# Routing attention and a hard-swish FFN on one core: band steps, the last pair's slots, two loads and an output queue rearranged

## The chip, the core and the metric

One core of a Trainium2 chip runs the kernel. TensorE (PE) multiplies matrices and writes to PSUM, VectorE (DVE), ScalarE (ACT) and GpSimd (POOL) work on tiles, SyncE (SP) issues DMAs; ACT and POOL issue some as well. Each engine takes its instructions in the order in which the program lists them, and waits where one needs what another engine or a DMA has not yet delivered. The metric is the device time of one execution in microseconds (us), as a median of several runs.

## The reference

```python
batch, n_heads, seq, head_dim, n_clusters = 4, 8, 768, 64, 16
q_assign = argmax(einsum('bhsd,hcd->bhsc', q_n, c_n), axis=-1)     # nearest centroid of each query
k_assign = argmax(einsum('bhsd,hcd->bhsc', k_n, c_n), axis=-1)     # and of each key
mask = q_assign[..., :, None] == k_assign[..., None, :]
scores = where(mask, q @ k.T / sqrt(64), -1e9)
attn = softmax(scores) @ v                                          # (4, 8, 768, 64)
x = attn.transpose(0, 2, 1, 3).reshape(3072, 512)
h = x @ w_in                                                        # (3072, 2048)
out = (h * clip(h + 3, 0, 6) / 6) @ w_out                           # (3072, 512)
```

A query attends to the keys of its own cluster only; then a feed-forward network runs over all 3072 tokens. All is float32.

## The kernel before

The 32 heads are worked on as 16 pairs (two heads of 64 dimensions fill 128 partitions). Four pairs make a batch of the attention's output, and a batch of the FFN can start when its four pairs are done.

**First part, the main loop.** Pairs 0 to 6 are computed in full width: a loop over steps `n` (two at a time, 12 to a pair) issues scores (L423, PE), exponentials (L446, ACT), sums over the keys (L454 and L457, POOL) and the product with v (L467, PE). In the same loop the FFN's weights are loaded as raw 512 KB pieces on SP's queue (`load_weights`, L232) and decoded (`decoding_steps`, L245 to L276, on ACT and DVE); each piece's `split` asks for the piece two further on. When batch 0's four pairs are done, their key sums are inverted and the first FFN block is loaded: `load_sums` appends `invert` and then `complete` to the list `later`, which is run once in each turn of the loop, and `complete` calls `load_block`, which issues the block's x (`xb`, L577) and its inverse sums (`rb`, L581) on SP. `divide` (L531, DVE) multiplies the two; the first `ph` matmuls (L656) need its result.

**Second part, the plan of items.** Pairs 7 (`FIRST`) to 15 go another way. Their tokens are ranked by cluster, the rows of q, k and v are scattered to DRAM in ranked order, and then only a band about the diagonal has to be computed. For each pair `steps_of` lists steps with an offset, and `late_plan` puts each step at item `i = 38 + 29 * (pair - 8) + offset`. The steps in question are

- ranking: `load_natural`, `turn_natural`, `cluster_scores`, `own_clusters`, `run_up`, `step_up` (L1071, DVE), `order` (L1106, L1119, PE), `positions`, and `scatter` (L1155, indirect DMAs that POOL issues);
- band: `load_ranked`, `turn_ranked`, three `band_scores` (L1228, PE; exponentials at L1250 and L1264, ACT), two `band_values` (L1285, PE), `key_adds` (L1299, DVE), `band_sums` (`pd`, L1309, PE, copied to `dn` by ACT at L1314), `band_divide` (`pdt` at L1322 and `ps` at L1326 on PE, then DVE);
- back in natural order: `keep_ranked` (L1343, SP), `gather` (L1198, twelve indirect DMAs on POOL), and `turn_back`, which transposes the gathered rows (`turn_piece`, L1038, PE), copies them to `xt` (L1039, ACT) and stores them to DRAM (L1353, SP).

After the steps of item `i` the loop issues one half-item of the FFN from the list `fill`, but none where `(i - 38) % 29` is 6 or 9. `turn_back` of a batch's last pair adds that batch's FFN items to `fill`.

**The FFN.** Each of the 4 batches has 3 blocks of 256 tokens, each block 8 `up` items and 7 `down` items of two halves. In `up`, `uX` (first half) and `uY` (second half) are matmuls at L709, with precomputed sums of weights `tx` that ACT's queue loads (L595, 384 KB) two items ahead; ACT and DVE then make the gate (L538, L541, L699, L720, L727). In `down`, `X` and `Y` are matmuls at L748; DVE adds the parts (L755) and `keep` (L761) writes the output in pieces of 128 KB, on SP's queue unless it is told otherwise.

**Buffers that matter.** In the second part the PSUM pool `psum_s` has a single buffer, which `turn_back` (L1038), `band_scores` (L1228) and `band_divide` (L1326) share. The pool `rowp` (tiles `xn`, `bn`, `xr`, `xt`) has three buffers.

**The end.** After the last step of the plan, `turn_back(15)`, `st["last"]` is set, `whether_good` puts a chain of small checks on DVE, and the rest of `fill` runs: what is left of batch 2, then batch 3.

Of the kernel before, what the change touches and what calls it, by code (L numbers as in the profile page):

```python
# [16 lines left out]
B, H, S, D = 4, 8, 768, 64  # L17
# [7 lines left out]
NPAIR = NG // 2  # L25
# [21 lines left out]
FIRST = NPAIR // 2 - 1  # L47
# [78 lines left out]
def fast_path(ctx, tc, ok, q, k, v, centroids, moe_w_in, moe_w_out, out):  # L126
# [380 lines left out]
    def load_sums(b):  # L507
        size = 2 * NCH
        tok = plain[:, NKT * b * size : (NKT * b + unsorted(b)) * size]
        nc.sync.dma_start(tok, st["sums", b].rearrange("k t s -> (k t s)").rearrange("(p n) -> p n", p=P))  # L510

        def invert():
            nc.vector.reciprocal(out=tok, in_=tok)
            nc.sync.dma_start(st["rd", b].rearrange("k t s -> (k t s)").rearrange("(p n) -> p n", p=P), tok)
            return complete

        def complete():
            if unsorted(b) == NKT:
                waiting.extend((b, m) for m in range(NHC))
                load_block()  # L520

        if b == 0:
            later.append(lambda: later.append(lambda wait=invert(): later.append(wait)))
        else:
            st["invert"], st["complete"] = invert, complete

# [108 lines left out]
    def ffn_items(b):  # L635
# [121 lines left out]
        def down(m, part):  # L757
# [33 lines left out]
            def end():  # L791
                multiply(1)
                if part == 0:
                    finish()
                    st["gating"] = False
                if (b, m, part) == (B - 1, NHC - 1, 6):
                    st["good"] = nc.values_load(ok[0:1, 0:1], min_val=0, max_val=1)
                if part == 4:
                    token_sums(*divmod(b * NHC + m + 1, NHC))
                y0, y1 = st["y0"], st.get("y1")  # L800
                if part == 1:
                    nc.scalar.copy(out=y0[:, HC:], in_=st["X"][:, HC:])
                    add(y0[:, HC:], y0[:, HC:], st["X"][:, 0:HC])
                elif part == 3:
                    add(y1[:, 0:HC], y0[:, HC:], st["Y1"][:, HC:])
                    add(y1[:, HC:], y1[:, 0:HC], st["Y"][:, 0:HC])
                    keep(1, 1, y1[:, HC:])
                elif part == 4:
                    nc.scalar.copy(out=y0[:, 0:HC], in_=st["X"][:, 0:HC])
                    keep(0, 0, y0[:, 0:HC])  # L810
                elif part == 5 and closing:
                    z = sxp.tile([P, 4, P], F32, name="sx").rearrange("p k c -> p (k c)")[:, 0:HC]
                    add(z, y0[:, HC:], st["Y"][:, 0:HC])
                    keep(0, 1, z)
                elif part == 6:
                    add(y1[:, 0:HC], y0[:, HC:], st["Y1"][:, HC:])
                    keep(1, 0, y1[:, 0:HC])
                    if not closing:
                        add(y0[:, HC:], y0[:, HC:], st["Y"][:, 0:HC])
                        keep(0, 1, y0[:, HC:], nc.scalar if st["last"] else nc.sync)  # L820
                if (b, m) == (0, 0):
                    for i in ([HF - 1, HF - 2], [5], [4], [], [3, 2], [0], [1])[part]:
                        make_first_sums(i)
                    if part in (0, 1):
                        weight_sums(6 + part)
                    elif part in (2, 3):
                        weight_sums(2 + part)
# [114 lines left out]
    def open_late():  # L942
# [2 lines left out]
        late = ctx.enter_context(ExitStack())  # L945
        for name, bufs in (
            ("rankp", 1), ("piecep", 2), ("svp", 1), ("fromp", 1), ("sortp", 1), ("bandp", 2), ("edgep", 1),
            ("wholep", 1), ("rowp", 3), ("posp", 3),
        ):
            st[name] = right(late, name, bufs)  # L950
        for name, bufs in (("psum_y", 2), ("psum_s", 1)):
# [409 lines left out]
    def steps_of(g):  # L1361

        first, last = g == SECOND, g == NPAIR - 1
        if first:
            plan = [
                (-38, load_queries), (-38, load_keys, 0), (-38, load_keys, 1),
            ]
        elif g == FIRST:
            plan = [(-6, lambda g: st.pop("signed")())]
        else:  # L1370
            plan = [
                (-52, load_natural, 1), (-51, load_natural, 0), (-46, turn_natural, 1), (-45, turn_natural, 0),
                (-42, cluster_scores), (-40, own_clusters), (-39, load_queries), (-39, run_up), (-38, step_up),
                (-36, load_keys, 0), (-35, order), (-34, positions), (-33, load_keys, 1),
            ]
        s = -37 if first else -30
        if g == FIRST:
            plan += [
                (-5, load_ranked, 0), (-4, load_ranked, 1), (-3, load_ranked, 2), (-5, band_masks),
                (-1, turn_ranked, 0), (0, turn_ranked, 1),  # L1380
            ]
        else:
            plan += [
                (s, scatter, 0), (s, scatter, 1), (-12, band_masks), (-9, load_ranked, 0),
                (-7, load_ranked, 1), (-6, load_ranked, 2), (-4, turn_ranked, 0), (-3, turn_ranked, 1),
            ]
        if last:
            plan += [
                (1, band_scores, (0, 5), 1), (2, band_scores, (2,), 3), (3, band_scores, (4,)),
                (3, band_values, 0), (3, key_adds, 0, 1, 2), (4, key_adds, 0, 3), (5, band_values, 1),  # L1390
                (5, key_adds, 1, 1, 2), (6, key_adds, 1, 3), (8, band_sums), (9, band_divide), (10, keep_ranked),
                (11, gather), (24, turn_back),
            ]
        else:
            plan += [
                (2, band_scores, (0, 5), 1), (4, band_scores, (2,), 3), (6, band_scores, (4,)),
                (6, band_values, 0), (6, key_adds, 0, 1, 2), (7, key_adds, 0, 3), (9, band_values, 1),
                (9, key_adds, 1, 1, 2), (10, key_adds, 1, 3), (12, band_sums), (14, band_divide), (16, keep_ranked),
                (17 if g == FIRST else 23, gather), (37, turn_back),
            ]  # L1400
        return [(g, *step) for step in plan]

    def late_plan():

        at = {}
        for g in range(FIRST, NPAIR):
            for _, offset, op, *args in steps_of(g):
                i = (AHEAD + SLOT * (g - SECOND) - 2 * (g == NPAIR - 1) if g > FIRST else 6) + offset
                assert i >= 0, (g, offset)
                at.setdefault(i, []).append((op, g, *args))  # L1410
        return [at.get(i, []) for i in range(max(at) + 1)]
# [85 lines left out]
    with tc.manual_schedule():  # L1497
# [24 lines left out]
        for n in range(0, total + lag_d + 2, 2):  # L1522
# [19 lines left out]
                prep.pop(0)()  # L1542
            if r == 6:
                load(g + 2, "q", "k")
                load(g + 1, "v")
            if len(prep) > 1:
                prep.pop(0)()
# [410 lines left out]
```

## Time and profile before

| | us |
|---|---|
| median of 3 runs | 925.34 |
| lowest, highest | 924.95, 927.41 |
| the profiled execution | 924.17 |
| its span | 922.4 |
| PE busy in it | 895.6 |
| POOL, DVE, ACT busy in it | 600.1, 586.4, 305.0 |
| mean granted clock of PE | 0.996 |

The profile shows one execution. Its page gives for each engine the busy time and its share of the span. Further views list what each engine waited for and for how long; the instructions in order of time, with the idle time before each in brackets and whoever ended it; the clock granted to PE in any window; and the chain of work that ended last. A row such as `PE ps L1038` names the engine, the tile written and the line. PE weight loads (PEld) overlap the matmuls, and so do neighbouring matmuls a little.

### The profile page before, as it was taken

Reading aid. Unit: us, or ns where it says so; the run is one execution under the profiler, and the core shown is the slowest. Engines: PE = TensorE matmul, PEld = TensorE weight load, DVE = VectorE, ACT = ScalarE, POOL = GpSimd, SP = SyncE. Lnnn points to the kernel's source line nnn. Section 1 sums busy time; section 2 is a strip of 40 time slices with the busy share of each in tenths; the row PEclk is TensorE's granted clock in tenths of the full one; section 3 lists DMA queues with packets and bytes.
Section 4 is the critical chain, followed back from the end, with each engine's and each line's share of the span. In section 5 each row is a group of like instructions: output and inputs, shape, how many; then the busy total and the mean of one; then the engine's idle time right before and its main releaser. Section 6 shows DMA issues by size and latency. Waiting matters only on the chain.

```text
span 922.4 us, 17421 instructions
## 1 busy us (share of the span) xinstructions
PE 895.6 (97%) x6131; PEld 701.4 (76%) x6131; DVE 586.4 (64%) x1373; ACT 305.0 (33%) x627; POOL 600.1 (65%) x1438
## 2 busy tenths in 40 slices
PE   8999999999999999999999999999999988999997
PEld 5444444657798797887977978978888878999996
DVE  5874898799787394693774855856744716445361
ACT  6888786651220322212222230321412201112120
POOL 3878899996867858787888777787886051203030
PEclk9999999999999999999999999999999999999999
DMA  6656666536769577593792954937635413233220
GB/s 178 169 154 170 174 186 186 160 98 136 199 165 197 134 182 152 151 238 89 185 216 79 223 110 140 236 102 172 160 108 132 122 42 111 88 83 102 63 64 28
DMA packets 248377, 131.06 MB, mean 142 GB/s; under 512 B 206972, under 2 KB 225816, under 8 KB 248280
## 3 DMA queue, kind: packets, MB, share of 16 engines
q1 hardware_dynamic: 224168, 81.22, 36.9%
q10 hardware_dynamic: 13744, 34.44, 13.5%
q0 software_dynamic: 10368, 14.18, 5.1%
q8 instruction: 51, 0.84, 0.4%
q14 instruction: 46, 0.38, 0.1%
HBM read 99.82 MB, written 29.97 MB: 141 GB/s over the span
## 4 chain that ended last, share of the span: by engine, by line
PE 48%; DVE 9%; DMA 4%; POOL 2%; issue 1%; ACT 1%; ACTq 0%; SPq 0%; DVEq 0%; POOLq 0%
PE Y L748 14%; PE uY L709 9%; PE X L748 9%; PE uX L709 8%; PE pv L1285 3%; PE ps L1228 2%; DMA tx<-td 2%; DVE g_sb L720 1%; DVE sx L720 1%; DVE g_sb L699 1%; DVE g_sb L541 1%; POOL xn L1198 1%; PE pv L1228 1%; PE pd L1309 1%; PE ps L1038 1%
## 5 line engine op out<-in xcount | busy, mean ns | idle before, releaser
L1198 POOL DMA_INDIRECT xn<-xsd,pos x108 | 106.7, 988 | 58.9 <-DMA xsd<-xr 29.3
L538 ACT ACTIVATE sx<-g_sb,half_c 128x512 f32<-128x512 f32 x88 | 63.6, 722 | 198.5 <-DVE g_sb L720 198.3
L1147 POOL MEMSET unread<- 128x1 f32 x972 | 102.3, 105 | 37.6
L699 POOL TENSOR_TENSOR g_sb<-g_sb 128x256 f32<-128x256 f32 x52 | 39.6, 783 | 118.7 <-DVE g_sb L541 117.6
L457 POOL TENSOR_TENSOR acc<-acc,ex 128x768 f32<-128x768 f32 x56 | 104.5, 1867 | 16.7 <-ACT ex L446 14.1
L1155 POOL DMA_INDIRECT qd<-qn,pos x96 | 98.1, 1022 | 20.0 <-issue 14.4
L1155 POOL DMA_INDIRECT kvd<-kvn,pos x96 | 95.5, 995 | 21.8 <-issue 21.8
L748 PE MATMUL X<-w_out_sb,g_sb 128*128 128x256 f32 x384 | 93.3, 387 | 1.5 <-DVE g_sb L541 1.4
L709 PE MATMUL uX<-xb,w_in_sb 128*128 128x128 f32 x704 | 93.0, 275 | 0.0
L748 PE MATMUL Y<-T,g_sb 128*128 128x256 f32 x384 | 88.5, 381 | 0.0
L748 PE MATMUL Y<-w_out_sb,g_sb 128*128 128x256 f32 x384 | 88.5, 381 | 0.0
L709 PEld LDWEIGHTS uX<-xb,w_in_sb 128*128 128x128 f32 x704 | 85.7, 192 | 0.0
L748 PEld LDWEIGHTS X<-w_out_sb,g_sb 128*128 128x128 f32 x384 | 71.7, 193 | 16.3 <-DVE g_sb L541 3.9
L748 PEld LDWEIGHTS Y<-w_out_sb,g_sb 128*128 128x128 f32 x384 | 72.2, 190 | 12.6 <-issue 2.7
L748 PEld LDWEIGHTS Y<-T,g_sb 128*128 128x128 f32 x384 | 72.0, 190 | 12.5 <-issue 2.7
L755 DVE TENSOR_TENSOR y<-y,Y 128x256 f32<-128x256 f32 x47 | 19.7, 420 | 92.7 <-PE Y L748 91.9
L720 DVE TENSOR_TENSOR sx<-uX,sx 128x128 f32<-128x128 f32 x176 | 50.7, 288 | 38.3 <-ACT sx L727 34.1
L423 PE MATMUL ps<-xf 64*128 64x384 f32 x336 | 68.8, 487 | 0.6 <-ACT ex L446 0.6
L720 DVE TENSOR_TENSOR g_sb<-uY,sx 128x128 f32<-128x128 f32 (+1 forms) x176 | 65.5, 413 | 0.2 <-DVE sx L720 0.2
L446 ACT ACTIVATE ex<-ps 128x768 f32<-128x768 f32 x84 | 63.7, 803 | 3.1 <-PE ps L423 2.6
L541 DVE SCALAR_TENSOR_TENSOR g_sb<-sx,g_sb 128x512 f32<-128x512 f32 x88 | 63.3, 722 | 2.0 <-ACT sx L538 2.0
L467 PE MATMUL pv<-ex,vt 128*64 128x384 f32 x336 | 63.5, 499 | 0.0
(228 smaller groups left out, 1723.7 us busy)
## 6 DMA issues: line engine op xcount, KB each, us to landing
tx<-td ACTq DMA_DIRECT2D x86, 384.0 KB
raw<-in_moe_w_in_dram SPq DMA_DIRECT2D x16, 512.0 KB
raw<-in_moe_w_out_dram SPq DMA_DIRECT2D x16, 512.0 KB
xb<-xd SPq DMA_DIRECT2D x12, 512.0 KB
out_dram<-y SPq DMA_DIRECT2D x44, 128.0 KB
piece<-qd SPq DMA_DIRECT2D x36, 96.0 KB
piece<-kvd SPq DMA_DIRECT2D x36, 96.0 KB
vs<-kvd SPq DMA_DIRECT2D x18, 192.0 KB
```

The costliest lines, as they stand in the source:

```text
L423: nc.tensor.matmul(st["ps", n][:, t, 0:HALF], lhsT=x[r, NCH + j], rhs=x[r, hf * NHC : (hf + 1) * NHC], start=first, stop=last, skip_group_ ...
L446: nc.scalar.activation(out=ex, in_=sc, func=ACT.Exp, scale=SM_SCALE)
L457: nc.gpsimd.tensor_tensor(out=acc, in0=acc, in1=ex, op=ALU.add)
L467: nc.tensor.matmul(pv[t * D : (t + 1) * D], lhsT=vt[:, t, j], rhs=ex[:, t], start=(j == 0), stop=(j == NCH - 1),)
L538: nc.scalar.activation(out=r, in_=h, func=ACT.Relu, bias=half_c, scale=1.0 / 6.0)
L541: nc.vector.scalar_tensor_tensor(out=g, in0=r, scalar=1.0, in1=h, op0=ALU.min, op1=ALU.mult)
L709: nc.tensor.matmul(dst, lhsT=w[:, kt], rhs=x(kt), start=(kt == 0), stop=(kt == HK - 1))
L720: nc.vector.tensor_tensor(out=out_, in0=in0, in1=in1, op=ALU.add)
L748: nc.tensor.matmul(bank[:, half * HC : (half + 1) * HC], lhsT=g_sb[:, kind, i], rhs=w[:, i], start=(first and i == 0), stop=(last and i == ...
L1147: nc.gpsimd.memset(unread, 0.0)
L1155: i = nc.gpsimd.indirect_dma_start(out=rows[name, g, t], in_=src[:, j, t].rearrange("p a d -> p (a d)") if a else src[:, j, t], in_offset= ...
L1198: nc.gpsimd.indirect_dma_start(out=xn[:, j, t], out_offset=None, in_=rows["xsd", g, t], in_offset=bass.IndirectOffsetOnAxis(ap=pos[:, 0, j ...
```

## The change

- The first block's loads: `invert` and `complete` of batch 0 go one level deeper into `later`, so that `complete`, and with it the loads of `xb` and `rb`, runs one turn of the loop later.
- `load(g + 1, "v")` runs at `r == 8` of a pair instead of `r == 6`.
- The output half (0, 1) of a block's last part goes to ACT's queue if its batch is the last, and not whenever the plan has ended.
- `rowp` has four buffers.
- Pair 8's base is 35 instead of 38, with offsets changed so that its loads and scatter stay where they were; its other steps come three items sooner.
- Pairs 9 to 15: the ranking up to `step_up` comes one item sooner; `load_queries`, `load_keys`, `order`, `positions` and `scatter` stay.
- All pairs but the last: `band_sums` at 11 (was 12), `band_divide` at 13 (was 14), `keep_ranked` at 14 (was 16), pair 7's `gather` at 15 (was 17), `turn_back` at 35 (was 37).
- The last pair: its steps with an offset above -20 are shifted by -4, where all its steps were shifted by -2; those before lose that shift. `turn_back(15)` gets offset 26 instead of 24 and stays at the same item.

```diff
         if b == 0:
-            later.append(lambda: later.append(lambda wait=invert(): later.append(wait)))
+            later.append(lambda: later.append(lambda wait=invert(): later.append(lambda: later.append(wait))))
...
-                        keep(0, 1, y0[:, HC:], nc.scalar if st["last"] else nc.sync)
+                        keep(0, 1, y0[:, HC:], nc.scalar if b == B - 1 else nc.sync)
...
-            ("wholep", 1), ("rowp", 3), ("posp", 3),
+            ("wholep", 1), ("rowp", 4), ("posp", 3),
...
         if first:
             plan = [
-                (-38, load_queries), (-38, load_keys, 0), (-38, load_keys, 1),
+                (-35, load_queries), (-35, load_keys, 0), (-35, load_keys, 1),
             ]
...
-                (-52, load_natural, 1), (-51, load_natural, 0), (-46, turn_natural, 1), (-45, turn_natural, 0),
-                (-42, cluster_scores), (-40, own_clusters), (-39, load_queries), (-39, run_up), (-38, step_up),
+                (-53, load_natural, 1), (-52, load_natural, 0), (-47, turn_natural, 1), (-46, turn_natural, 0),
+                (-43, cluster_scores), (-41, own_clusters), (-40, run_up), (-39, load_queries), (-39, step_up),
                 (-36, load_keys, 0), (-35, order), (-34, positions), (-33, load_keys, 1),
             ]
-        s = -37 if first else -30
+        s = -34 if first else -30
...
         if last:
...
-                (11, gather), (24, turn_back),
+                (11, gather), (26, turn_back),
             ]
         else:
             plan += [
                 (2, band_scores, (0, 5), 1), (4, band_scores, (2,), 3), (6, band_scores, (4,)),
                 (6, band_values, 0), (6, key_adds, 0, 1, 2), (7, key_adds, 0, 3), (9, band_values, 1),
-                (9, key_adds, 1, 1, 2), (10, key_adds, 1, 3), (12, band_sums), (14, band_divide), (16, keep_ranked),
-                (17 if g == FIRST else 23, gather), (37, turn_back),
+                (9, key_adds, 1, 1, 2), (10, key_adds, 1, 3), (11, band_sums), (13, band_divide), (14, keep_ranked),
+                (15 if g == FIRST else 23, gather), (35, turn_back),
             ]
...
-                i = (AHEAD + SLOT * (g - SECOND) - 2 * (g == NPAIR - 1) if g > FIRST else 6) + offset
+                i = offset + {FIRST: 6, SECOND: 35}.get(g, AHEAD + SLOT * (g - SECOND))
+                if g == NPAIR - 1 and offset > -20:
+                    i -= 4
...
             if r == 6:
                 load(g + 2, "q", "k")
+            if r == 8:
                 load(g + 1, "v")
```

## The prediction

> **What bounds the kernel now.** I read the page's first part, then the list of waits for TensorE (PE), then the timeline around each long wait, then clock and busy time by windows.
>
> ```profile
> span 922.4 us, 17421 instructions
> PE 895.6 (97%) x6131; PEld 701.4 (76%) x6131; DVE 586.4 (64%) x1373; ACT 305.0 (33%) x627; POOL 600.1 (65%) x1438
> ...
> PE ps L1038 <- DMA xn<-xsd,pos: 3.4, 3, 1.2
> ...
> PE ps L423 <- ACT ex L446: 2.9, 4, 2.1
> PE rk L1106 <- DVE upto L1071: 2.5, 3, 1.4
> ...
> PE ps L1228 <- ACT be L1250: 0.3, 1, 0.3
> ```
>
> The last four rows are: engine and line, what it waited for, us in total, times, longest. PE is busy for 895.6 of 922.4 us, so 26.8 us idle are all that a reordering can win, and PE's instructions stay the same 6131. A wait taken from PE shortens the run by its length, a new one lengthens it; what DVE (VectorE), ACT (ScalarE), POOL (GpSimd) and the DMAs do counts only where PE waits for it. The sum goes against this profiled execution, 924.17 us (its span and 1.77 us around it). The median of the runs, 925.34, is 1.17 above it; I add the difference that I find to the median.
>
> **The change part by part.** One ended wait is worth a little more than the row says: two neighbouring PE pieces overlap (the row 728.13 0.82 below ends at 728.95, the next starts at 728.79), so 0.16 us of overlap come back with it.
>
> *A, first block later.* The x and 1/sum loads of the first block (xb, rb) go behind two raw weight loads on SP's queue.
>
> ```profile
> 131.06 0.38 SPq L232 DMA_DIRECT2D raw<-in_moe_w_out_dram  x1
> 131.97 0.53 SPq L577 DMA_DIRECT2D xb<-xd  x1
> 134.82 3.97 SPq L232 DMA_DIRECT2D raw<-in_moe_w_out_dram  x2
> 144.08 0.67 ACT L245 ACTIVATE wsize<-raw 128x512 bf16<-128x512 f32 x1 [2.82 <-DMA raw<-in_moe_w_out_dram]
> 145.49 1.22 DVE L531 TENSOR_TENSOR xb<-xb,rb 128x1024 f32<-128x1024 f32 x1
> 145.59 0.34 PE L423 MATMUL ps<-xm 64*128 64x384 bf16 x2 [2.13 <-ACT ex L446]
> 149.54 1.78 PE L656 MATMUL ph<-xb,w_in_sb 128*128 128x256 f32 x7
> ...
> raw<-in_moe_w_out_dram SPq DMA_DIRECT2D x5, 512.0 KB
> xb<-xd SPq DMA_DIRECT2D x1, 512.0 KB
> rb<-rd SPq DMA_DIRECT2D x2, 256.0 KB
> ...
> xd<-num SPq DMA_DIRECT2D x2, 192.0 KB
> ```
>
> Times are us from the span's start; in brackets the idle time before and who ended it. The raw load issued at 134.82, behind xb and rb, reaches ACT only at 144.08; the exponentials queued behind it on ACT come late, and PE stands 2.13 us. With both raw loads first that ends: −2.3 with the overlap. What is late next is the first block. From 131.06 to 144.08 the queue brought raw, the 192 KB of xd, xb, rb and raw, 2240 KB in 13.0 us, or 3.0 us for 512 KB. The second raw load, issued by 138.79, is in at about 141.5, xb and rb 6.0 us later, at 147.5. The division (1.22 us) ends at 148.7, while the first `ph`, now at 149.54, would be due 2.3 earlier, at 147.25. So it waits 1.4: A = −0.9. Bounds: −2.3 if the loads are quicker, +2.1 if another 512 KB lie ahead of them. Queued behind the division on DVE is the decoding of weights, for which ACT and the next raw load wait; that is inside the upper bound.
>
> *B, ranking one item sooner.* `run_up` and `step_up` (DVE) go ahead of the half-item after which `order` (PE) stands.
>
> ```profile
> 286.69 0.25 PE L1106 MATMUL rk<-every,upto 128*128 128x1 bf16 x4 [1.37 <-DVE upto L1071]
> 402.42 0.25 PE L1106 MATMUL rk<-every,upto 128*128 128x1 bf16 x4 [0.45 <-DVE upto L1071]
> 461.88 0.25 PE L1106 MATMUL rk<-every,upto 128*128 128x1 bf16 x4 [0.63 <-DVE upto L1071]
> ```
>
> A half-item lasts 1.34 us or more (728.79 to 730.13 in the rows below), enough for each but the first, of which a rest may stay. 1.37 + 0.45 + 0.63, three overlaps (0.48), less 0.1: B = −2.8, between −2.0 and −2.9.
>
> *C and D, the end of the last pair.* An item now lies between `band_sums` and `band_divide` of pair 15. Its band steps come two items sooner; `turn_back(15)` stays.
>
> ```profile
> 725.31 0.55 PE L1322 MATMUL pdt<-ident,dn 128*128 128x128 f32 x3 [0.60 <-ACT dn L1314]
> 726.34 0.61 PE L709 MATMUL uY<-xs,tx 128*128 128x128 f32 x4
> 728.13 0.82 PE L1038 MATMUL ps<-ident,xn 128*128 128x128 f32 x6
> 728.79 0.61 PE L709 MATMUL uX<-xs,tx 128*128 128x128 f32 x4
> 728.99 0.80 ACT L1039 COPY xt<-ps 128x768 f32<-128x768 f32 x1 [3.73 <-PE ps L1038]
> 729.68 0.72 ACT L538 ACTIVATE sx<-g_sb,half_c 128x512 f32<-128x512 f32 x1
> 730.13 0.61 PE L709 MATMUL uY<-xs,tx 128*128 128x128 f32 x4
> 730.24 0.38 SPq L1343 DMA_DIRECT2D xsd<-xr  x1
> 755.11 0.47 PE L1038 MATMUL ps<-ident,xn 128*128 128x128 f32 x1 [1.07 <-DMA xn<-xsd,pos]
> 755.38 3.38 PE L748 MATMUL X<-w_out_sb,g_sb 128*128 128x256 f32 x8
> ```
>
> The copied sums (dn) get a half-item of cover: C = −0.8. For D, the chain from `turn_back(14)` (728.13) over keep (730.24) and POOL's gathers to the last transposes (755.11) is as long as before, and PE runs out of work before its end: the 3.4 us of the first waits row. By the changed order one uY half-item more, 726.34 to 728.13 or 1.79 us, lies inside that stretch: D = −1.8, with some 1.6 of wait left; bounds −1.5 and −3.4.
>
> *E, the early output.* In block 2 of batch 2 the last half row goes out on SP's queue, not ACT's. By the changed order it is the only DMA that changes queue; loading v two steps later moves none.
>
> ```profile
> 770.78 0.35 ACTq L761 DMA_DIRECT2D out_dram<-y  x1
> 770.80 0.71 PE L709 MATMUL uY<-xs,tx 128*128 128x128 f32 x4 [0.68 <-DVE y L755]
> 771.22 0.41 ACTq L595 DMA_DIRECT2D tx<-td  x1
> 774.59 0.68 PE L709 MATMUL uX<-xs,tx 128*128 128x128 f32 x4 [1.73 <-DMA tx<-td]
> ```
>
> The load of `tx` stands behind that output on ACT, and the output waits for DVE's sum, as uY does; PE waits 1.73 us for `tx`. Without it ACT can issue `tx` well before: E = −1.9; bounds 0 and −1.9. On SP nothing that PE needs soon stands behind the output.
>
> *F, the price of sooner sums.* `turn_back(g−1)` moves from offset 37 to 35, that is 29 + 6: the same item as `band_scores(g, (4,))`. Both write the one bank of `psum_s`. In the changed order six pairs of them, (7,8) and (9,10) to (13,14), stand back to back on PE, with a wait for ACT between; now something lies between everywhere, and the waits show only 0.3 us at L1228. The nearest rows are those of `turn_back(14)`: the transposes start at 728.13, the next PE work could start at 728.79, ACT's copy out of the bank ends at 729.79. So PE would lose 1.0 us at each: F = +6.0. Bounds: 0, if the copy were hidden, and 12.8, if an `sx` activation and a `tx` issue stand ahead on ACT (0.72 at 729.68, 0.41 at 771.22).
>
> The Trainium skill speaks against this part of the change: "Perfetto Trace Analysis", section "Optimizing Tensor Performance", subsection "Matmuls", says that independent matmul groups should rotate through different PSUM banks, so that ACT's or DVE's evacuation overlaps the next group's matmuls. Two groups in one bank break that; by the rule the sum holds F, by the trace of before alone, which has no such wait, it would be without F. No run shown so far settles it.
>
> *G, sums before their adds.* `band_sums` (pd) stands one item nearer to the key additions on DVE.
>
> ```profile
> 257.22 0.61 PE L709 MATMUL uY<-xs,tx 128*128 128x128 f32 x4
> 257.55 0.38 DVE L1299 TENSOR_TENSOR bw<-bw,be 128x224 f32<-128x224 f32 x1
> 319.83 1.77 DVE L1299 TENSOR_TENSOR bw<-bw,be 128x480 f32<-128x480 f32 x3
> 321.44 0.61 PE L709 MATMUL uY<-xs,tx 128*128 128x128 f32 x4
> ```
>
> For pair 7 pd would start where uY is now, 257.22, while the last addition ends at 257.93: 0.7. For pair 8, 321.60 against 321.44: 0.2. The other pairs have more room. G = +0.9, between 0 and 3.
>
> The fourth buffer of `rowp` and pair 8's earlier loads take away buffer waits off PE; nothing on PE waited for them, and POOL's scatter and gather calls (65% busy) cover them: 0.
>
> Sum: −0.9 − 2.8 − 0.8 − 1.8 − 1.9 + 6.0 + 0.9 = −1.3.
>
> **The rivals.** (1) F is hidden, because ACT's copy keeps pace with the transposes: −7.3, so 918.0. For it: PE has no such wait now. Against: one bank, and a copy of 0.80 us that starts only after the last transpose (728.99 against 728.95). (2) Slower: the same bank costs more. If ACT has an activation and a DMA issue ahead of the copy, each place costs 1.0 + 0.72 + 0.41 = 2.13 us, F = 12.8 and the sum +5.5: 930.8. It decides above (7.3 + 2.8) / 6 = 1.7 us a place. Against it: ACT had stood idle for 3.73 us before that copy. (3) A turns round: the first block's loads come 3.0 us later still, A = +2.1, the sum +1.7: 927.0. For it: the division heads DVE's queue, and the raw load after it waits behind it. Then the first part doesn't do what it says. (4) The clock:
>
> ```profile
> 755.00:758.00 3.00, 2.89 (x8) 2.35 (x9) 0.00 (x0) 0.80 (x1) 0.00 (x0) 0.50 0.25 101
> ...
> 535.62 3.46 PE X L748 x16
> ```
>
> The first row is a window: us, then busy time and instructions of PE, weight loads, DVE, ACT and POOL, then the granted clock, 0.50 after the three waits. Eight X matmuls take 3.38 us there (755.38) where 16 take 3.46 elsewhere (second row, of the chain that ended last), so 1.65 are lost. With the shorter wait the drop may go, and 1.65 more with it, if all of it counts: 922.4. Against: uY at 770.80 already waits 0.68 for DVE, whose chain starts with the transposes, not with X. "TensorE: Matmul & The Clock Gate", Part 1 of the Trainium skill, halves the clock after an idle window of about 3.4 us; the trace agrees (0.50), and by it the drop would go.
>
> **How the numbers follow.** Within 0.3%, 2.8 us, is about what a measurement can't tell from no change. Forecast: −1.3 on the median, so 924.0; its own range is 921 to 927, A's bounds for the most part. Its chance is 0.48 (faster 0.16, same 0.31, slower 0.01). Rival 1: 0.22, all faster. Rival 2: 0.16, all slower. Rival 3: 0.09 (same 0.06, slower 0.03). Rival 4: 0.05 (faster 0.03, same 0.02). Together: faster 0.41, same 0.39, slower 0.20. The range, 917.5 to 928.5, takes in most of rival 1 and the forecast's and rival 3's own spread, and leaves rival 2 out.
>
> **What would show it.** Right: PE L1228 waits for ACT's xt copy (L1039) six times, near 1 us each; the rows at 286, 402, 462, 725 and 774 are gone; `ps L423 <- ACT ex` loses its 2.1, and `ph` waits for xb; the transposes of pair 15 wait about 1.6 us in all and the clock stays at 1.0. Wrong: no wait at L1228 (rival 1), waits there over 1.5 us (rival 2), or new waits at L423 or L656 of 3 us and more (rival 3).

## The result: 0.8% slower, and the profile after

| | before | changed |
|---|---|---|
| median of 11 runs, us | 924.95 | 931.38 |
| lowest, highest | 922.02, 927.41 | 927.96, 940.46 |
| profiled execution, its span | 924.17, 922.4 | 932.76, 930.9 |
| PE busy in it | 895.6 | 896.5 |

The ratio is 1.0082, with a 95% interval of 1.0055 to 1.0109: 7.6 us slower, 5.1 to 10.1. PE did the same work; it stood idle for 34.4 us instead of 26.8. Where, the list of PE's waits of the changed kernel tells (engine and line, what it waited for, us in total, times, longest; "issue" means that the profile names nothing that the engine waited for):

```profile
PE ps L1228 <- ACT xt L1039: 5.3, 6, 0.9
PE X L748 <- DVE g_sb L541: 2.8, 7, 0.9
PE ph L656 <- DVE xb L531: 2.7, 1, 2.7
PE uX L709 <- DVE g_sb L699: 2.2, 2, 1.5
PE ps L1038 <- issue: 2.2, 1, 2.2
PE uY L709 <- DVE y L755: 1.8, 1, 1.8
...
PE uX L709 <- DVE sx L720: 1.4, 1, 1.4
...
PE ps L423 <- ACT ex L446: 1.0, 4, 0.3
PE ps L1038 <- DMA xn<-xsd,pos: 0.9, 1, 0.9
PE uX L709 <- DVE upto L1071: 0.7, 1, 0.7
PE uX L709 <- DVE xs L632: 0.7, 1, 0.7
...
PE uX L709 <- DMA tx<-td: 0.3, 1, 0.3
```

All the waits that the change was forecast to remove are gone: rk for `upto` (2.5), pdt for `dn` (0.6), the 2.1 of the scores, the 1.7 for `tx`. The six bank waits are there, 0.89 us each where the forecast had 1.0. Three things were not in the forecast, or much smaller there: X and uX wait 7.3 us in all for VectorE's gate, ranking additions and `sx` (before: 1.7), `ph` waits 2.7 for the division, and `turn_back(14)` waits 2.2.

The first block, in the timeline and in windows of the changed kernel (a window's row: us, its length, then busy time and instructions of PE, weight loads, DVE, ACT, POOL; granted clock; DMA share; GB/s):

```profile
146.11 2.71 DVE L531 TENSOR_TENSOR xb<-xb,rb 128x1024 f32<-128x1024 f32 x1 [2.58 <-DMA rb<-rd]
148.97 5.38 PE L656 MATMUL ph<-xb,w_in_sb 128*128 128x256 f32 x16 [2.74 <-DVE xb L531]
...
149.00:152.00 3.00, 3.00 (x9) 2.45 (x10) 2.90 (x4) 0.00 (x0) 2.84 (x3) 0.62 0.22 48
152.00:155.00 3.00, 3.00 (x14) 2.04 (x15) 2.93 (x4) 0.62 (x2) 2.81 (x5) 0.81 0.85 262
```

The loads were in at 146.1, earlier than the forecast 147.5. But the division took 2.71 us and not 1.22, and behind the wait the granted clock fell to 0.62, so that the sixteen `ph` matmuls took 5.38 us; at full clock they take 3.69 (the control run c1 below).

The end of the last pair, in the timeline of the changed kernel:

```profile
733.07 0.49 PE L1322 MATMUL pdt<-ident,dn 128*128 128x128 f32 x3
733.40 0.82 PE L1326 MATMUL ps<-ident,bn 128*128 128x128 f32 x6
734.14 0.68 DVE L541 SCALAR_TENSOR_TENSOR g_sb<-sx,g_sb 128x512 f32<-128x512 f32 x1
734.86 1.56 DVE L699 TENSOR_TENSOR g_sb<-g_sb 128x256 f32<-128x256 f32 x4
736.33 0.22 DVE L1330 RECIPROCAL inverses<-pdt 128x12 f32<-128x12 f32 x1
736.66 1.02 DVE L1333 TENSOR_TENSOR xr<-ps,inverses 128x384 f32<-128x384 f32 x2
737.78 0.96 PE L1038 MATMUL ps<-ident,xn 128*128 128x128 f32 x6 [2.23 <-issue]
...
740.03 1.09 SPq L1343 DMA_DIRECT2D xsd<-xr  x2
...
763.77 0.33 PE L1038 MATMUL ps<-ident,xn 128*128 128x128 f32 x1 [0.90 <-DMA xn<-xsd,pos]
773.39 0.71 PE L709 MATMUL uX<-xs,tx 128*128 128x128 f32 x4 [0.65 <-DVE xs L632]
779.97 0.38 PE L709 MATMUL uY<-xs,tx 128*128 128x128 f32 x1 [1.84 <-DVE y L755]
```

pdt waits for nothing now, but the item that gives it cover also puts that item's gate work (L541, L699) on VectorE ahead of the division (L1330, L1333). The division reads the bank of `psum_s`, so `turn_back(14)` waits 2.23 us for it; the row names "issue", but PE's last step before it was done at 735.6 and the division ended at 737.7. One long wait has moved from the gathered rows to the bank. Behind uY's wait of 1.84 us the granted clock was 0.54 in the window from 781 to 783 us, and 0.60 in the next 2 us.

### The profile page after: what moved, and what is told of

It is laid out like the page before. It is cut to its first block, busy times and chain, and to the rows that moved or that the text cites. A ratio compares the mean times of both kernels' runs of the same rounds, so it can differ in the third digit from the quotient of the medians.

```text
span 930.9 us, 17381 instructions
## 1 busy us (share of the span) xinstructions
PE 896.5 (96%) x6131; PEld 702.3 (75%) x6131; DVE 592.2 (64%) x1373; ACT 305.6 (33%) x627; POOL 599.8 (64%) x1438
## 4 chain that ended last, share of the span: by engine, by line
PE 74%; DVE 10%; DMA 5%; POOL 5%; ACT 3%; issue 2%; SPq 0%; DVEq 0%; POOLq 0%; ACTq 0%
PE Y L748 16%; PE uY L709 11%; PE X L748 11%; PE uX L709 8%; PE ps L423 6%; PE pv L467 5%; POOL xn L1198 3%; PE pv L1285 3%; PE ph L656 3%; PE ps L1228 3%; DVE g_sb L699 2%; DVE g_sb L541 1%; DVE g_sb L720 1%; PE pv L1228 1%; POOL unread L1147 1%
## 5 line engine op out<-in xcount | busy, mean ns | idle before, releaser
L699 POOL TENSOR_TENSOR g_sb<-g_sb 128x256 f32<-128x256 f32 x52 | 38.9, 769 | 120.1 <-DVE g_sb L541 119.1
L720 DVE TENSOR_TENSOR sx<-uX,sx 128x128 f32<-128x128 f32 x176 | 50.7, 288 | 38.7 <-ACT sx L727 34.2
L1299 DVE TENSOR_TENSOR bw<-bw,be 128x480 f32<-128x480 f32 (+1 forms) x54 | 30.6, 568 | 55.7 <-ACT bw L1264 28.6
L720 DVE TENSOR_TENSOR g_sb<-uY,sx 128x128 f32<-128x128 f32 (+1 forms) x176 | 65.5, 413 | 0.0
L541 DVE SCALAR_TENSOR_TENSOR g_sb<-sx,g_sb 128x512 f32<-128x512 f32 x88 | 63.6, 725 | 2.0 <-ACT sx L538 2.0
```

The costliest lines, as they stand in the source:

```text
L541: nc.vector.scalar_tensor_tensor(out=g, in0=r, scalar=1.0, in1=h, op0=ALU.min, op1=ALU.mult)
L699: eng.tensor_tensor(out=out_, in0=in0, in1=in1, op=op)
L720: nc.vector.tensor_tensor(out=out_, in0=in0, in1=in1, op=ALU.add)
```

## The experiments

Each run is set against runs of the kernel before on the same chip. Chips differed (medians of before 932.22 for e1 to e4, 931.89 for c1, e5, e6 and e7, 935.59 for e8 to e11, 925.58 for c2, e12, e13 and e14), so only ratios are compared, and 0.1% is 0.93 us. "Changed" is the changed kernel.

| run | ratio to before | 95% interval |
|---|---|---|
| first measurement of the change | 1.0082 | 1.0055 to 1.0109 |
| c1 changed, second chip | 1.0113 | 1.0041 to 1.0184 |
| c2 before itself | 1.0006 | 0.9979 to 1.0034 |
| e1 changed, turn_back late | 1.0015 | 0.9987 to 1.0044 |
| e2 changed, block early | 1.0124 | 1.0075 to 1.0174 |
| e3 changed, ranking late | 1.0140 | 1.0094 to 1.0185 |
| e4 before + queue | 0.9977 | 0.9948 to 1.0007 |
| e5 before + turn_back sooner | 1.0025 | 0.9993 to 1.0058 |
| e6 before + ranking sooner | 1.0066 | 1.0027 to 1.0106 |
| e14 before + run_up, step_up sooner | 1.0009 | 0.9981 to 1.0036 |
| e9 before + block late | 1.0016 | 0.9979 to 1.0053 |
| e10 before + sums, division, keep sooner | 1.0069 | 1.0029 to 1.0109 |
| e12 before + sums, division sooner | 1.0042 | 1.0015 to 1.0070 |
| e13 before + keep sooner | 1.0014 | 0.9984 to 1.0043 |
| e8 changed, bank and tail mended | 1.0049 | 1.0014 to 1.0084 |
| e7 before + queue + sooner tail | 0.9941 | 0.9903 to 0.9979 |
| e11 e7 + turn_back(15) sooner | 0.9906 | 0.9872 to 0.9940 |

### Controls

c1 is the changed kernel as it is, c2 the kernel before as it is.

> The changed kernel itself, as a control beside the next three: a ratio of 1.005 to 1.011 to the kernel before, as first measured, with six waits of 0.89 us at L1228 for the xt copy, a wait of about 2.7 us of ph for the division and one of 2.2 us of turn_back(14)'s transposes. If the ratio here is 1.012 or more, the chip weighs such waits differently, and the runs of one chip must not be set against another's.

Its ratio has an upper end beyond what was expected. The bank waits and the 2.23 us ahead of `turn_back(14)` are the same to the hundredth, but `ph` waited 0.80 us at full clock, where the first profile had 2.74 and a fallen clock. So a wait that hangs on a DMA's landing can differ between executions of one kernel by 3.6 us, 1.9 of waiting and 1.7 of clock; the bank waits don't differ.

> The kernel before itself, as a control: ratio 1.000 within its interval, which is the noise of this comparison (0.997 to 1.003 expected). Its profile should show the waits that every kernel has on this chip: about 2.2 us at rk of pair 8, 1 to 3 us of uX near 600 us, which belong to no edit. If the ratio is off by 0.4% or more, the sizes of the single edits are not to be trusted beyond their sign.

1.0006, within what was expected: the comparison is good to about 0.3%. Of the waits that it should show, rk of pair 8 was 0.5 and uX near 600 us 1.1; these differ by the run too. rk of pair 8 (near 208 us, ahead of most edits) waits 2.1 to 2.3 us in the profiles of e4, e7, e10, e11 and e12, about 0.5 in c2, e6, e13 and e14, and not at all in the others. So single profiles differ by some 2 us that belong to no edit.

### The bank

e1, from the changed kernel:

```diff
-                (15 if g == FIRST else 23, gather), (35, turn_back),
+                (15 if g == FIRST else 23, gather), (37, turn_back),
```

> The changed kernel with turn_back of all pairs but the last at offset 37 again, the rest of the change kept. Theory of the bank: the six waits of PE at L1228 for ACT's xt copy (0.89 us each, 5.3 in all, with the lost overlap about 6) are the price of this offset alone; they vanish and the time falls by 5 to 6.5 us against the changed kernel, to about 925.5 (ratio to before about 1.001). Rival, the DVE queue: PE only runs sooner into VectorE's backlog, so that the waits of uX and X for DVE grow and half or less of it comes back: 1 to 3 us, about 929.

No wait for xt is left, and the ratio is 1.0015, as the bank theory had it (1.001); the interval lies wholly below that of the first measurement, though against c1 the two just touch. In this profile two other long waits stand, 4.1 us (pd of pair 7 for the key sums, behind a stall of VectorE told of at the end) and 3.8 us (uX for VectorE).

e5, from the kernel before (with `rowp` at four buffers):

```diff
-                (17 if g == FIRST else 23, gather), (37, turn_back),
+                (17 if g == FIRST else 23, gather), (35, turn_back),
```

> The kernel before with turn_back of all pairs but the last at offset 35 (and rowp with four buffers), nothing else of the change. Theory of the bank: each place where turn_back's transposes stand directly ahead of a band_scores gets a wait of 0.89 us at L1228 for the xt copy, 5 to 6 us in all, ratio about 1.006. Rival, the DVE queue: the waits come, but VectorE catches up in them, so that waits of uX and X for DVE shrink and the time rises by 3 us or less.

The waits came, six of 0.89 us, but the ratio rose by 0.25% only, 2.3 us; the 1.006 of the bank theory lies just outside the interval. That is the size which the rival named, but not for its reason: X and uX wait 1.5 us for VectorE in this profile, against 1.7 before. What fell are the three waits for the gathered rows (3.4 us), which are gone. The timelines of before and of this run, around the last pair's division and keep:

```profile
726.54 1.02 DVE L1333 TENSOR_TENSOR xr<-ps,inverses 128x384 f32<-128x384 f32 x2
...
729.81 0.33 SPq L1353 DMA_DIRECT2D xd<-xt  x1
730.24 1.25 SPq L1343 DMA_DIRECT2D xsd<-xr  x2
```

```profile
738.18 0.33 SPq L1353 DMA_DIRECT2D xd<-xt  x1
...
739.94 1.02 DVE L1333 TENSOR_TENSOR xr<-ps,inverses 128x384 f32<-128x384 f32 x2 [0.42 <-PE ps L1326]
740.99 0.96 SPq L1343 DMA_DIRECT2D xsd<-xr  x2
...
763.32 0.82 PE L1038 MATMUL ps<-ident,xn 128*128 128x128 f32 x6
```

Before, keep (xsd) left SP 2.7 us after `xr` was ready (727.56), because the store of pair 14 (xd) stood ahead of it on SP and waited for its own transposes. With `turn_back(14)` ahead of the division keep leaves 0.03 us after, and the gathers follow: `turn_back(15)` at 763.32 waits for nothing.

### The first block

e2, from the changed kernel:

```diff
-            later.append(lambda: later.append(lambda wait=invert(): later.append(lambda: later.append(wait))))
+            later.append(lambda: later.append(lambda wait=invert(): later.append(wait)))
```

e9 is the reverse, on the kernel before.

> The changed kernel with the first block's loads one turn earlier again, as before. Theory: the later loads cost more than they won, a 2.74 us wait of ph for the division and 1.66 us in which the ph matmuls run at a lower granted clock behind that wait, against the 2.13 us stall of the scores that they end; undone, the time falls by 2 to 2.5 us against the changed kernel, ph starts without a wait, its sixteen matmuls take 3.7 us again and the stall of 2.1 us at L423 is back. Rival, the prediction's term: undone, the time rises by 0.9 us.

The waits did as expected: `ph` waits no more, and the scores stand 2.73 us again. But no 2 us came back (1.0124, beside the 1.0113 of c1), and tx waits of 5.1 us and one of 4.5 for pair 7's key sums stood elsewhere. Behind the 2.73 us the granted clock fell to 0.50 here (146 to 149 us), so the old order can pay for a fallen clock too; in e5, which has it as well, the clock was 0.50 from 145 to 147 us behind a wait of 2.16. Inconclusive.

> The kernel before with the first block's loads one turn later, nothing else. Theory: the stall of 2.1 us at L423 goes, ph waits 0.8 to 2.8 us for the division, and in some executions the granted clock falls behind that wait (1.7 us more): between 1 us faster and 2.5 us slower, ratio 0.999 to 1.003. The prediction's term: 0.9 us faster, ratio 0.999.

1.0016: neither a gain nor a loss can be told from no change. The profile says why the size is not to be had. In this execution:

```profile
148.55 1.78 DVE L531 TENSOR_TENSOR xb<-xb,rb 128x1024 f32<-128x1024 f32 x1 [5.38 <-DMA rb<-rd]
...
150.00:153.00 3.00, 2.51 (x7) 2.08 (x8) 2.90 (x5) 0.00 (x0) 2.88 (x5) 0.64 0.51 119
```

The loads came 2.4 us later than in the changed kernel's first profile, `ph` waited 4.62 us and the clock fell to 0.64. Six profiles have the late loads; `ph` waited 0.68, 0.80, 2.74, 2.76, 2.78 and 4.62 us in them. The sixteen `ph` matmuls end between 150.3 and 155.9 us there (mean 152.9), and between 150.7 and 154.2 in the twelve profiles with the early loads (mean 151.8). The later loads seem to cost about 1 us, less than either order scatters.

### The ranking

e3, from the changed kernel:

```diff
-                (-40, run_up), (-39, load_queries), (-39, step_up),
+                (-39, load_queries), (-39, run_up), (-38, step_up),
```

e6 moves the whole ranking up to `step_up` one item sooner in the kernel before, e14 only `run_up` and `step_up`, both for pairs 9 to 14. (In the change itself pair 15 loses its old shift by -2, so that its ranking comes an item later; no run tries that alone.)

> The changed kernel with run_up and step_up of pairs 9 to 15 one item later again, which moves work on VectorE alone; PE's order stays. Theory of the DVE queue: the ranking additions are in front of the gate's work wherever they stand; the waits at rk come back (about 2.5 us) and those of X and uX for DVE (7.1 us in the changed kernel) fall by as much or more, so that the time is within 1.5 us of the changed kernel's, or up to 3 us lower. Rival, the prediction's term: the rk waits come back and nothing falls, 2.8 us slower.

The rk waits came back (2.1 us), and those for VectorE did not fall in this profile (X 2.9, uX 5.2). So, by this profile, most of what X and uX wait for VectorE in the changed kernel doesn't come from the sooner additions. Beside c1 the 1.0140 is no difference that the intervals can tell. Neither theory is borne out by it.

> The kernel before with the ranking of pairs 9 to 14 up to step_up one item sooner (the last pair's is left, as two of its tiles would wait for one another), nothing else. Theory of the DVE queue: the three waits at rk go (2.5 us), and VectorE's gate work for the next FFN item, now behind the ranking additions, makes uX or X wait about as long: the time stays within 1.5 us of before (ratio 0.9985 to 1.0015). The prediction's term: 2.8 us faster, ratio 0.997.

> The kernel before with run_up and step_up of pairs 9 to 14 one item sooner and nothing else: only VectorE's order changes. Theory of the DVE queue: the rk waits go, the gate's work comes later by as much, ratio 0.999 to 1.003. The prediction's term: 0.997. Rival, that VectorE's order alone made the sooner ranking slow: ratio 1.005 or more.

e14 decides the term: the only difference is VectorE's order, the rk waits of pairs 9 to 14 are gone, and the time is the same (1.0009; the forecast 0.997 lies outside the interval). What stands in their place, the profiles of c2 and of e14 show, one chip. Both run the same 6131 matmuls in the same order, so they can be set side by side one by one. First c2:

```profile
PE rk L1106 <- DVE upto L1071: 2.5, 3, 1.4
PE uX L709 <- DMA tx<-td: 1.6, 3, 1.1
PE X L748 <- DVE g_sb L541: 1.6, 5, 0.5
...
460.03 0.33 ACTq L595 DMA_DIRECT2D tx<-td  x1
464.17 0.68 PE L709 MATMUL uX<-xs,tx 128*128 128x128 f32 x4 [0.19 <-DMA tx<-td]
```

Then e14:

```profile
PE uX L709 <- DMA tx<-td: 4.4, 4, 2.3
PE X L748 <- DVE g_sb L541: 2.3, 6, 0.9
...
282.24 0.70 PE L748 MATMUL X<-w_out_sb,g_sb 128*128 128x256 f32 x2 [0.92 <-DVE g_sb L541]
460.54 0.33 ACTq L595 DMA_DIRECT2D tx<-td  x1
464.60 0.68 PE L709 MATMUL uX<-xs,tx 128*128 128x128 f32 x4 [1.64 <-DMA tx<-td]
```

X and `tx` waits grew by 3.5 us, and at each of the three rankings it can be followed what became of the gain. At pair 9, X just ahead of rk now waits 0.92 for the gate work that the additions have pushed back: e14 is 0.54 us ahead of c2 before that X, 0.81 behind in it, and 0.54 ahead again at rk, so nothing is won. At pair 11, 0.5 us are won at rk and lost again at the next uX, which waits for `tx`. At pair 12, 0.7 are won at rk and 1.4 lost at uX: ACT issues the `tx` load behind an `sx` activation, which waits for the gate on VectorE, and the load goes out at 460.54 instead of 460.03. Another 1.15 us of the growth, a `tx` wait near 593 us, lie at no ranking.

e6 was slower, by 2.5 to 9.8 us, where no change was expected. As e14 was not (on another chip; the two intervals just touch), its loss lies most likely in what e6 has besides: the loads of the natural rows, the transposes and PE's cluster steps one item sooner. Which of them was not tried.

### The sums

```diff
-                (9, key_adds, 1, 1, 2), (10, key_adds, 1, 3), (12, band_sums), (14, band_divide), (16, keep_ranked),
-                (17 if g == FIRST else 23, gather), (37, turn_back),
+                (9, key_adds, 1, 1, 2), (10, key_adds, 1, 3), (11, band_sums), (13, band_divide), (14, keep_ranked),
+                (15 if g == FIRST else 23, gather), (37, turn_back),
```

That is e10. e12 has the sums at 11 and the division at 13 alone; e13 has keep at 15 and pair 7's gather at 16 alone.

> The kernel before with band_sums, band_divide, keep_ranked and the first gather of all pairs but the last at the changed offsets, turn_back left at 37. The prediction's term: 0.9 us slower, 0.7 of it as a pd of pair 7 that waits for the last key addition. Rival: the divisions now stand behind other FFN work on VectorE, 2 to 4 us slower, ratio 1.002 to 1.004.

> The kernel before with band_sums at 11 and band_divide at 13, keep and gather left. Theory of the DVE queue: the division's VectorE work now stands ahead of an FFN item's gate work instead of behind it, and the gate is what PE waits for next: 3 to 6 us slower, ratio 1.003 to 1.007. Rival, the gathers: no change within the noise, ratio 0.998 to 1.002.

> The kernel before with keep_ranked and pair 7's gather one item sooner, sums and divisions left; TensorE's, VectorE's and ScalarE's order is the same. Theory of the DVE queue: no change within the noise, ratio 0.998 to 1.002. Rival, the gathers: POOL's and SP's queues shift against the tx and piece loads and cost 3 to 6 us, ratio 1.003 to 1.007.

e10 cost 6.4 us (2.7 to 10.1), e12 3.9 (1.4 to 6.5), e13 nothing that can be told. So the sums and divisions carry most of it, on VectorE and PE; the queues of keep and gather were tried by one item only, where e10 moves them by two. In e12 the timeline shows what the forecast priced, and a second part:

```profile
259.43 1.52 PE L1309 MATMUL pd<-bw,ones 128*32 128x384 f32 x8
...
259.67 0.38 DVE L1299 TENSOR_TENSOR bw<-bw,be 128x224 f32<-128x224 f32 x1
...
264.56 1.55 DVE L699 TENSOR_TENSOR g_sb<-g_sb 128x256 f32<-128x256 f32 x4
...
266.55 0.22 DVE L1330 RECIPROCAL inverses<-pdt 128x12 f32<-128x12 f32 x1
266.88 1.02 DVE L1333 TENSOR_TENSOR xr<-ps,inverses 128x384 f32<-128x384 f32 x2
...
275.23 0.85 PE L356 MATMUL pcs<-xnat,cnT 128*32 128x384 f32 x8 [0.59 <-DVE xnat L1016]
```

pd spans 1.52 us instead of 0.85, because half of its matmuls wait for the addition that ends at 260.05: 0.67 inside a row that shows as busy. The division now stands behind the gate sums (L699) and not ahead of them, as e10's rival had it and not as e12's theory did; the next pair's transposes on VectorE come later, and PE waits 0.59 for them. The full 3.9 us are not in this profile. Its span is 4.6 us above that of c2, but it had fallen behind by 2.7 before the first moved step ran, mostly at rk of pair 8 (2.13 us against 0.49) and by a lower clock behind it. About 2 us are left for the edit there; 3.9 stands on the runs alone.

### The queue and the tail

The first pair of lines is e4, from the kernel before; e7 has all of it; e11 has `turn_back` at 25 instead of 26. The last two lines come on top of the old shift by -2.

```diff
-                        keep(0, 1, y0[:, HC:], nc.scalar if st["last"] else nc.sync)
+                        keep(0, 1, y0[:, HC:], nc.scalar if b == B - 1 else nc.sync)
...
-                (5, key_adds, 1, 1, 2), (6, key_adds, 1, 3), (8, band_sums), (9, band_divide), (10, keep_ranked),
-                (11, gather), (24, turn_back),
+                (5, key_adds, 1, 1, 2), (6, key_adds, 1, 3), (8, band_sums), (8, band_divide), (9, keep_ranked),
+                (10, gather), (26, turn_back),
...
+                if g == NPAIR - 1 and offset > -20:
+                    i -= 2
```

> The kernel before with one edit, the last half row of block 2 of batch 2 on SP's queue. Theory: the wait of 1.73 us for tx at the second up item of batch 3 is gone and nothing takes its place, 1.9 us faster than before (ratio 0.998). Rival: the division of labour behind it decides, the next wait is for VectorE's y sum and the checks, and the time stays.

2.1 us faster by the ratio, as forecast, though the interval just takes in no change. In its profile the wait of uX for `tx` behind the first up item of batch 3 is gone; uY before it waits 1.69 us for the y sum, where it was 0.68. So part of the gain may go there, as the rival had it; uY's wait differs between profiles of the kernel before, too (0.03 in c2).

> The kernel before with the queue edit, and with the last pair's band steps, sums, keep and gather two items sooner as in the change, but with band_divide in the same item as band_sums, so that no gate work of the FFN comes between them on VectorE; keep follows one item later, ahead of turn_back(14), which stays at offset 37. Theory of the tail: the 2.2 us wait ahead of turn_back(14) in the changed kernel came from band_divide's VectorE work standing behind an FFN item's; here it does not appear, the three waits for the gathered rows (3.4 us) and that for tx (1.7) go, the waits for VectorE after turn_back(15) come to 2 to 2.5 us: 4 to 5.5 us faster than before, ratio about 0.995. Rival: the chain behind turn_back(15) takes all of it back, no change beyond the queue edit's 1.9 us.

5.5 us faster (1.9 to 9.0). The timeline has the steps: the division follows pdt at once (733.52), keep goes at 735.22, ahead of the store of pair 14, and the transposes of pair 15 don't wait.

```profile
733.52 0.23 DVE L1330 RECIPROCAL inverses<-pdt 128x12 f32<-128x12 f32 x1 [0.62 <-PE pdt L1322]
734.17 1.02 DVE L1333 TENSOR_TENSOR xr<-ps,inverses 128x384 f32<-128x384 f32 x2 [0.42 <-PE ps L1326]
735.22 0.97 SPq L1343 DMA_DIRECT2D xsd<-xr  x2
...
738.88 0.82 PE L1038 MATMUL ps<-ident,xn 128*128 128x128 f32 x6
...
761.34 0.82 PE L1038 MATMUL ps<-ident,xn 128*128 128x128 f32 x6
...
771.65 0.71 PE L709 MATMUL uX<-xs,tx 128*128 128x128 f32 x4 [0.87 <-DVE xs L632]
```

Behind them uX waits 0.87 and uY 1.85 us for VectorE, 2.7 in all, a little more than expected.

> The kernel before with the queue edit and the sooner tail (ratio 0.994), and turn_back(15) one item sooner. Theory: the gathered rows land about 2 us ahead of it there, so that it comes 1.7 us sooner with a wait of 0 to 0.5 us; the chain behind it (store, xb, checks) starts sooner and the waits for VectorE at 771 and 778 us, 2.7 in all, fall to about 1: 1 to 1.7 us faster than that kernel, ratio 0.992 to 0.993. Rival: the rows land later than it, and it waits as long as it gained.

0.9906: 5.6 to 11.8 us faster than before, the lowest ratio of this study and lower than expected, though its interval overlaps with that of e7. Its transposes of pair 15 start without a wait, and neither uX nor uY waits for VectorE behind them.

> The changed kernel with turn_back back at 37 and with the last pair's band_divide in the same item as its band_sums and keep one item later: its bank waits and its tail are mended, the first block's loads, the ranking, the sums and pair 8 are left as changed. Beside the kernel before with that tail and the queue edit alone (ratio 0.994). Theory: the sooner ranking and the later loads cost what was measured, so this stands 4 to 9 us above that, ratio 0.998 to 1.004. Rival, the prediction's terms for the rest (-0.9, -2.8, +0.9): 2.8 us below it, ratio 0.991.

1.0049, just above the expected 0.998 to 1.004 and far from the rival's 0.991: what is left of the change, first block, ranking, sums and pair 8, costs time. Pair 8's sooner steps, put at 0 in the forecast, and the later load of v were not run alone.

## Why the prediction was wrong

Forecast 924.0 us, 1.3 faster; measured 7.6 slower. The waits that were to go went, and the bank waits that were to come came. What failed is the pricing: a wait of PE that ends was counted as gain, without asking where the work behind it goes and which wait comes next.

| term | forecast | rows of PE, after less before | single edit, us |
|---|---|---|---|
| A first block | -0.9 | -2.1 + 2.7 + 1.7 = +2.3 | e9: +1.5 (-1.9 to +4.9) |
| B ranking | -2.8 | -2.5; X and uX for VectorE +5.6, `tx` -1.0, neither of B alone | e14: +0.8 (-1.8 to +3.3); e6: +6.1 (+2.5 to +9.8) |
| C, D tail | -2.6 | -4.0 + 2.2 + 0.9 + 1.8 = +0.9 | |
| E queue | -1.9 | -1.7 | e4: -2.1 (-4.8 to +0.6) |
| F bank | +6.0 | +5.3 | e5: +2.3 (-0.6 to +5.4) |
| G sums | +0.9 | +0.7 | e10: +6.4 (+2.7 to +10.1); e12: +3.9 (+1.4 to +6.5) |

- **B is the step that failed most plainly.** Its -2.8 took the removed rk wait as gain, as if a half-item of PE's work were all that stands between. But the additions, put sooner, stand ahead of gate work that PE needs next. e14 shows it: the rk waits are gone, no gain (+0.8 us, -1.8 to +3.3), and what was won at the three rankings is lost at X and uX within 5 us of each. The bound of -2.0 was too narrow. The growth of X's and uX's waits for VectorE in the changed kernel, from 1.7 to 7.3 us, is not B's alone, as e3 keeps it without the sooner additions; which part of the change brings it stays open.
- **C and D.** "One uY half-item more lies inside that stretch: D = -1.8" counted PE's cover and left out what the uY item puts on VectorE: the gate work ahead of the division, 2.2 us at the bank. Without that item between, and with keep ahead of pair 14's store, e7 gains 5.5 us, where C, D and E together promised 4.5. The rows of the table leave the clock out: the drop behind the gathered rows (about 1.5 us) is gone, and one behind uY's 1.84 us costs about 1.0. The chain behind `turn_back(15)` takes part of the gain; with that step sooner as well, e11 has no such wait.
- **G was mis-sized.** Its 0.7 at pair 7 is there (0.67). That the moved divisions change VectorE's order for all pairs was not priced at all. With it sums and divisions cost 3.9 us in e12 (1.4 to 6.5), without the keep; its profile shows about 2.
- **A was mis-sized.** The landing was forecast rightly, 147.5 against 145.2 to 148.6 in six profiles. Not in the sum were a division of more than 1.2 us (up to 2.7) and a clock that falls behind the wait in some executions (three of the six), as it falls behind the old stall in some (e2, e5). In the first profile A came to +2.3, just beyond its upper bound of +2.1; as a term alone (e9) it can't be told from zero, nor from -0.9.
- **F and E were right in their mechanism.** Six places, 0.89 each; and the `tx` wait went. E's size lies within e4's interval, but so does zero. What F leaves out is that `turn_back` two items sooner also clears SP's queue for the last keep, if pair 14's store doesn't wait for the division; in the changed kernel it does.
- **The rivals.** Rival 1, a hidden copy, is out: the six waits are there. Rival 2, slower through a dearer bank, has the sign but not the cause: no place waited more than 0.89. Rival 3, the first block, is near the first profile's +2.3 for A, but that is about a fourth of the 8.6 us between the two first profiles; e9 can't settle it. Rival 4, the clock after the tail: the drop behind the transposes is gone (1.00 from 764 to 767 us), as it said, but uX and uY then wait 0.65 and 1.84 us for the same chain, with a drop of its own. The rival that was missing is VectorE as the bound of the ranking and division stretches, though it is busy only 64% of the span.

The single edits sum to more than the change (e5, e10, e6, e9 and e4 give 14 us, without the tail), but five such intervals together leave about 7 us of doubt, so whether they overlap isn't shown. How the extra of e6 and of e10 divides over single waits stays open.

## What to carry over

A wait removed on the bounding engine is a gain only if the engine that it waited for has nothing else that the bounding engine needs next: write down that engine's queue at the new place, instruction by instruction, before taking the wait off. In a tail chain look at what stands ahead in each queue it passes: a store on SP that waited for its own data held a ready one back by 2.7 us there, and putting the division and the keep ahead of foreign work gave more than the whole change was to give (e7). The bank with one buffer cost a wait of 0.89 us, about ACT's copy of 0.80, at each of the six places where two users touched; that price could be read off before (1.0).

## What the runs showed of the hardware that was not expected

- **The granted clock falls after shorter waits than the prediction had seen.** There it stood at 0.50 after three waits of 3.4 us together. A single wait of 2.74 us took it to 0.62 (changed), one of 2.78 had matmuls as slow (e3: 5.28 us for sixteen, clock 0.53), one of 2.16 took it to 0.50 (e5), and behind one of 1.84 it was 0.54 (changed). But one of 2.76 left it at 1.00 (e1: 3.69), and 2.13 us before the change did nothing. The Trainium skill, "TensorE: Matmul & The Clock Gate", Part 1, gives an idle window of about 3.4 us; here less was enough in some executions, and the same wait does not always do it.
- **One VectorE instruction took 1.22 to 2.71 us.** It is the division (L531) of 128x1024 elements, the same instruction in all eighteen profiles.
- **VectorE stood still with its input from PE there.** In e1 for 4.6 us and in e2 for 4.5, at the same place in the program (before L720 of pair 7's stretch); the trace names no engine or DMA of the kernel that it waited for, so another input isn't ruled out. In c1, with the same instructions there, it did not. The cause wasn't tried.
